# Attention with chunk selection and a gated FFN: key extremes ahead of the transposes, guard and mask as products, and a new order

## The chip, the cores and the metric

One core of a Trainium2 chip runs the whole kernel. The metric is device microseconds (us) of one execution, the lower the better; beside the measured time stands the span that the profiler shows on the core. The engines are PE (TensorE matmul, with its weight load PEld), DVE (VectorE), ACT (ScalarE), POOL (GpSimd) and SP (SyncE, which only issues DMAs here).

## The reference, cut to what matters

For 4 sequences of 768 tokens, 8 heads and 64 channels, each query scores the 24 chunks of 32 keys by an upper bound, keeps the six best, and attends causally to the keys of these chunks. The heads' outputs side by side (512 wide) go through a sigmoid-gated FFN with 1536 hidden units.

```python
k_min = np.min(k_chunks, axis=3)                  # chunks of 32 keys
k_max = np.max(k_chunks, axis=3)
ub = np.sum(np.maximum(q * k_min, q * k_max), axis=-1)      # per query and chunk
ub = np.where(causal, ub, -1000000000.0)          # chunks that begin behind the query
top_chunks = np.argsort(ub, axis=-1)[..., -6:]
scores = scale * np.matmul(q, k.transpose(0, 1, 3, 2))
mask = sel & (pos[:, None] >= pos[None, :])
attn = softmax(np.where(mask, scores, -1000000000.0))
x = (attn @ v).transpose(0, 2, 1, 3).reshape(B * S, H * D)
gate = 1.0 / (1.0 + np.exp(-(x @ w_gate)))
out = (gate * (x @ w_val)) @ w_out
```

## The kernel before, in words

**Stages.** The 3072 tokens go through nine stages. Sequence 0 takes the stages 0 (128 rows), 1 (256) and 2 (384), so that work begins on little data; the sequences 1 to 3 take two stages of 384 rows each (3 to 8). Each stage has a preparation (keys and queries turned so that channels lie on partitions, key extremes, bounds, selection), an attention part (scores, exp, product with v, normalising) and an FFN part.

**Order.** Every operation is a task with a name `kind:stage.number` and one or more engines that may run it. A string `ORDER` lists all tasks by name, with `/1` or `/2` where not the first engine is taken; they are issued in this order, and each engine runs its own instructions in it, as a queue. Buffers are rings of fixed length: `ld` has 6 loads, PSUM has two double banks `big` and four single banks `m`. The numbers in the code behind an engine's name are a planner's costs, which place filler matmuls and nothing else.

**Names.** `kch`, `qch`: loads of 128 keys or queries of sequence 0 (lines 455 and 460, on SP's queue or ACT's). `vn`, `v`: loads and casts of the values. `wst`, `w`: nine loads of the FFN's weights on POOL's queue (507, 509). `ps`: a small DMA that copies 25 pattern rows into the keys, which join the selection to the scores (407). `kTp`, `qT`: four fp32 transposes of 128x128 by PE (561). `kxn`: the minimum or maximum of chunks' keys (571); `kc`: what is left of it, the minimum and the difference to the maximum, into `kcat` (580 to 593). `hk`: keys as f16 into `headK` (604, 611). `Qc`: queries out of PSUM, once raw and once rectified, since the bound is q times minimum plus relu(q) times difference (522 on ACT, 526 on DVE); `hq`: their cast to f16 (537). `ub`: the matmuls of the bounds (733); `ubq`, `mx8`, `Ap`, `apT`, `mq`: causal penalty, the eight largest, the selection as rows of `headQ` (736 to 761). `sc`: scores (810), `at`: exp (815) and POOL's causal select on the diagonal block (821), `pv` (835), `xn` (848), `xtp`, `xT` (861, 866), `gv` gate and value matmuls (891), `gate` (901), `hglu` (903), `o` (917), `osb` (924), `out` (932).

**Stage 0** has only four chunks, so nothing need be selected for its first 128 queries, except where a bound is so large that the check on it, the guard, matters. `first_guard` computes the bounds, the largest bound less a constant (`guard`), transposes it by PE (708) and copies it as eight more rows under the queries (`first`); `firstK` holds the keys with eight constant rows (`less`) under them, so that the score matmul subtracts the guard with its 72 rows.

**Sequences 1 to 3** load keys and queries in 128-byte pieces on SP's queue (`kb`, `qb`, line 422, 192 KB each, four to a transpose). DVE turns them in 32x32 blocks (`kTt` 641, `Qct` 672), reduces (`kn`, `kx`, 646) and writes `kcat` (654, 655); `rl` (681, 683) makes relu of the queries in SBUF.

**Warm-up.** Where PE would wait in the first stages, `fill` (340) puts matmuls on zeros into its queue.

Of the kernel before, what the change touches and what calls it, by code (L numbers as in the profile page):

```python
# [17 lines left out]
LATENCY = {"PE": 0.22, "ACT": 0.08, "DVE": 0.06, "POOL": 0.12, "SP": 3.0, "Q0": 3.0, "Q2": 3.0}  # L18


ORDER = """
    c.0 kch.0 wst0.0 is.0 is.2 qch.0 c.2 w0.0 wst1.0 is.1 vn.0 c.3 vn.1 c.4 c.8/1 v.0 wst2.0 c.5 kTp:0.0 c.6 kch.1
    vn.2 qT:0.0 kxn:0.0 ps.0 kxn:0.1 Qc:0.1 qch.1 kc:0.0 wst3.0 w1.0 Qc:0.3 wst4.0 Qc:0.2 kch.2 hk:0.0 wst5.0 Qc:0.0
    hk:0.1 wst6.0 ubp:0.1 qch.2 hk:0.2/1 ubp:0.0 v.1 kTp:1.0 hk:0.3/1 c.9 qT:1.0 kxn:1.0 Ap:0.1 c.11 c.10 kxn:1.1
    Qc:1.1 wst7.0 w2.0 vn.3 gT:0.1/1 Qc:1.2/1 kTp:1.1 gT:0.0/1 sc:0.1 Qc:1.0/1 sc:0.0 at:0.2 kxn:1.3 Qc:1.3 at:0.3
    kxn:1.2 at:0.0 kc:1.0 qT:1.1 at:0.1 Qc:1.6 pl.0 hk:1.1 wst8.0 pv:0.3 pv:0.2 pv:0.6 pv:0.0 pv:0.1 Qc:1.4 xn:0.0
    w3.0 c.7 Qc:1.7 hk:1.2 xtp:0.0 pv:0.4 pv:0.7 pv:0.5 Qc:1.5 xn:0.1 hk:1.0/1 ub:1.0 Ap:0.0 xtp:0.1 ubq:1.0 hq:1.1
    xT:0.0/1 ubq:1.1 xT:0.1/1 mx8:1.0 hk:1.3/1 gv:0.6 kch.3 v.2 gv:0.0 qch.3 gv:0.7 Ap:1.0 hq:1.0/1 gv:0.1 w4.0 ub:1.1
    gv:0.8 kch.4 apT:1.0 gv:0.3 gv:0.2 gate:0.1 mq:1.3/2 v:0.0 ubq:1.2 sc:1.3 gate:0.0 mq:1.1 qch.4 ubq:1.3 at:1.6
    mx8:1.1 mq:1.0 sc:1.1 mq:1.2 gv:0.4 at:1.2 gv:0.5 Ap:1.1 sc:1.2 kch.5 at:1.4 sc:1.0 at:1.7 apT:1.1 mq:1.7/2 at:1.0  # L30
    mq:1.6/2 sc:1.7 mq:1.4/2 v.3 hglu:0.0 gv:0.9 gv:0.10 qch.5 at:1.14 sc:1.6 w5.0 at:1.3 pv:1.7 gv:0.11 at:1.1
    at:1.12 sc:1.4 at:1.5 pv:1.6 pv:1.1 mq:1.5 at:1.8 pv:1.4 pv:1.3 pv:1.2 pv:1.5 at:1.13 sc:1.5 xn:1.1 pv:1.0 at:1.9
    qT:2.0 at:1.10 at:1.15 hglu:0.1 kTp:2.0 c.13 at:1.11 xn:1.0 pv:1.14 gv:0.12 Qc:2.2 w6.0 gv:0.18 vn.4 gv:0.19
    gv:0.20 kxn:2.1 gv:0.13 c.14 gate:0.3 gv:0.14 vn.5 pv:1.9 pv:1.15 kxn:2.0 pv:1.13 gate:0.2 pv:1.10 pv:1.12 kTp:2.2
    vn.6 xn:1.3 Qc:2.0 kb:3.0 pv:1.8 pv:1.11 qT:2.2 xn:1.2 hk:2.0/1 xtp:1.0 w7.0 Qc:2.8/1 gv:0.15 Qc:2.3 gv:0.21
    xtp:1.1 xT:1.0 hk:2.1/1 gv:0.22 gv:0.23 xT:1.1 gv:0.16 gv:0.17 Qc:2.1 gv:1.0 hglu:0.2 kTp:2.1 gate:1.0 hglu:0.3
    gv:1.2 Qc:2.11 w8.0 kxn:2.2 gv:1.1 Qc:2.9 gv:1.4 hglu:1.0 gate:1.1 qT:2.1 kxn:2.5 gate:1.2 gv:1.12 Qc:2.6 kxn:2.4
    gv:1.3 gv:1.13 gate:1.6 hglu:1.1 Qc:2.5 gv:1.16 hglu:1.6 gv:1.5 kxn:2.3 gate:1.8 gv:1.10 Qc:2.10 gv:1.11 hglu:1.2
    Qc:2.4 gv:1.14 kc:2.0 gv:1.17 gate:1.5 hq:2.0 Qc:2.7 gv:1.18 hglu:1.5 hglu:1.8 gate:1.7 ub:2.0 v.4 gate:1.9 gv:1.6
    ubq:2.0 gv:1.19 kb:3.1 gate:1.3 ubq:2.1 ub:2.1 hk:2.2/1 mx8:2.0 o:0.0 kb:3.2 gv:1.7 hk:2.4/1 v.5 o:0.1 Ap:2.0  # L40
    hk:2.3/1 o:0.2 kb:3.3 o:0.3 apT:2.0 hk:2.5/1 o:0.4 mq:2.0/2 qb:3.0 v.6 o:0.5 hglu:1.9 mq:2.1 ubq:2.2 sc:2.0 mq:2.3
    gv:1.15 qb:3.1 hq:2.1 osb:0.0/1 at:2.0 sc:2.1 hglu:1.3 gv:1.20 at:2.2 qb:3.2 hglu:1.7 sc:2.3 at:2.1 ubq:2.3
    gv:1.21 mx8:2.1 gate:1.10 gv:1.8 qb:3.3 at:2.5 sc:2.2 Ap:2.1 gv:1.9 kb:3.4 gate:1.4 gv:1.22 mq:2.2 hglu:1.10
    at:2.3 sc:2.6 apT:2.1 kb:3.5 gv:1.23 gate:1.11 Qct:3.0 at:2.4 sc:2.4 at:2.9 pv:2.0 mq:2.4 kb:3.6 pv:2.4 pv:2.3
    hglu:1.4 pv:2.2 v:0.1 pv:2.1 at:2.6 sc:2.7 Qct:3.1 mq:2.5 kb:3.7 o:1.6 at:2.10 at:2.11 sc:2.5 kTt:3.0 vn:3.0
    pv:2.5 qb:3.4 o:1.7 at:2.8 xn:2.0 pv:2.11 at:2.7 sc:2.9 qb:3.5 mq:2.6 o:1.8 hglu:1.11 at:2.14 sc:2.8 mq:2.7 o:1.0
    qb:3.6 vn:3.1 at:2.12 pv:2.8 pv:2.9 pv:2.10 kTt:3.1 pv:2.7 sc:2.10 qb:3.7 rl:3.0 at:2.13 o:1.1 kn:3.0 c.12 o:1.9
    hq:3.0 kb:5.0 pv:2.6 pv:2.12 pv:2.13 at:2.15 sc:2.13 pv:2.14 kx:3.0 o:1.10 at:2.20 out:0.0 at:2.16 sc:2.12 kb:5.1
    o:1.11 at:2.18 sc:2.14 xn:2.1 o:1.2 at:2.21 o:1.3 kb:5.2 Qct:3.2 o:1.4 osb:1.1 sc:2.11 kc:3.0 o:1.5 at:2.17 kb:5.3
    sc:2.15 Qct:3.3 at:2.19 ub:3.0 at:2.23 at:2.22 pv:2.19 pv:2.17 qb:5.0 osb:1.0/1 pv:2.16 hk:3.0 pv:2.15 rl:3.1  # L50
    pv:2.20 pv:2.18 ubq:3.0 pv:2.22 pv:2.21 pv:2.23 xtp:2.0 xn:2.2 qb:5.1 hq:3.1 xT:2.0/1 xn:2.3 ubq:3.1 xtp:2.1
# [954 lines left out]
```

## Time and profile before

| | |
|---|---|
| median of three runs | 300.95 us (300.33 to 301.96) |
| the profiled execution | 300.8 us, span 298.8 us |
| granted clock of TensorE | 1.00 |
| busy in the span | PE 284.5, DVE 212.4, ACT 203.9, POOL 107.5 us |

A row of the timeline reads: start, duration (both us), engine, line, operation, output and input by the program's names, and how many instructions it groups; in brackets, the idle time before it and what ended it. Matmuls are pipelined, so that a busy PE isn't always a PE at its peak. A window's row gives start and end, length, then the busy time of each engine with the count of its instructions, the granted clock, the DMA share (the time that packets took on the 16 DMA engines, over the window's; it can pass 1) and GB/s.

### The profile page before, as it was taken

How to read it: one execution, taken by the hardware profiler on the slowest of the kernel's cores; microseconds unless marked ns; L12 is line 12 of the kernel's file. 1: busy time of each engine (PE TensorE's matmuls, PEld its weight loads, DVE VectorE, ACT ScalarE, POOL GpSimd, SP SyncE). 2: the span in 40 equal slices, each digit the busy share in tenths (PEclk: the TensorE clock that was granted, in tenths of full speed). 3: DMA queues.
4: the chain of work that ended last, by engine and by line, in shares of the span. 5: the costliest groups of instructions: out<-in, count | busy, mean ns of one | idle time of the engine just before them, and what ended most of it. 6: DMA issues, size and time to landing. Idle time of an engine off the chain costs nothing.

```text
span 298.8 us, 6823 instructions
## 1 busy us (share of the span) xinstructions
PE 284.5 (95%) x2642; PEld 181.2 (61%) x2642; DVE 212.4 (71%) x581; ACT 203.9 (68%) x299; POOL 107.5 (36%) x175
## 2 busy tenths in 40 slices
PE   6668998999999999999999999999999999999995
...
DMA  7999999999699273575790500006210000021012
GB/s 152 256 218 279 229 171 114 193 149 175 74 215 160 43 141 58 96 63 109 111 85 2 124 0 2 3 3 71 20 70 2 35 2 0 2 103 39 0 70 106
DMA packets 110072, 27.99 MB, mean 94 GB/s; under 512 B 100311, under 2 KB 105525, under 8 KB 110040
## 3 DMA queue, kind: packets, MB, share of 16 engines
q1 hardware_dynamic: 81608, 19.28, 31.5%
...
q10 hardware_dynamic: 1712, 0.66, 1.1%
...
q14 instruction: 12, 0.10, 0.1%
...
## 4 chain that ended last, share of the span: by engine, by line
PE 83%; DVE 8%; DMA 4%; ACT 2%; issue 1%; SPq 1%; DVEq 0%; ACTq 0%
PE m_o L917 21%; PE m_v L891 17%; PE m_g L891 16%; PE big_sc L810 12%; PE m_pv L835 6%; PE big_gv L891 5%; PE m_ub L733 4%; DMA ld_q<-in_q_dram 4%; PE m_xtp L861 2%; ACT Qcat L522 1%; DVE kxn L571 1%; DVE mx L749 1%; PE big_kqT L561 1%; ACT at L815 1%; DVE hglu L903 1%
## 5 line engine op out<-in xcount | busy, mean ns | idle before, releaser
L815 ACT ACTIVATE at<-big_sc 128x1024 f16<-128x1024 f32 (+3 forms) x96 | 84.7, 909 | 17.1 <-PE big_sc L810 11.6
L917 PE MATMUL m_o<-wo,hglu 128*128 128x512 f16 (+1 forms) x300 | 72.0, 370 | 0.0
L821 POOL TENSOR_SCALAR_AFFINE_SELECT at<-at 128x384 f16<-128x384 f16 (+2 forms) x66 | 33.3, 515 | 105.5 <-ACT at L815 101.6
L891 PE MATMUL m_v<-xT,wv 128*128 128x384 f16 (+2 forms) x384 | 71.2, 306 | 0.1
L891 PE MATMUL m_g<-xT,wg 128*128 128x384 f16 (+2 forms) x384 | 70.3, 306 | 0.0
L903 DVE SCALAR_TENSOR_TENSOR hglu<-gate,m_v 128x384 f16<-128x384 f16 (+1 forms) x88 | 44.9, 527 | 19.8 <-PE m_v L891 15.5
L901 ACT ACTIVATE gate<-m_g 128x384 f16<-128x384 f32 (+1 forms) x88 | 40.8, 477 | 24.4 <-PE m_g L891 20.3
L891 PEld LDWEIGHTS <-wg 128*128 128x128 f16 x432 | 38.7, 98 | 23.8 <-issue 4.4
L810 PE MATMUL big_sc<-headQ,headK 89*128 89x128 f16 (+2 forms) x472 | 51.6, 240 | 0.8 <-DVE headQ L761 0.6
L891 PEld LDWEIGHTS <-wv 128*128 128x128 f16 x432 | 38.6, 98 | 20.6 <-issue 0.9
L810 PEld LDWEIGHTS <-headK 89*128 89x128 f16 x472 | 33.4, 97 | 12.7 <-issue 1.1
L917 PEld LDWEIGHTS <-hglu 128*128 128x128 f16 x300 | 27.0, 98 | 22.7 <-issue 1.2
L835 PEld LDWEIGHTS <-at 128*128 128x128 f16 x672 | 30.2, 98 | 12.7 <-issue 1.9
L835 PE MATMUL m_pv<-v,at 128*128 128x65 f16 x672 | 34.0, 194 | 1.1 <-POOL at L821 1.1
L761 POOL COPY headQ<-apT 25x384 f16<-25x384 f16 (+1 forms) x30 | 14.7, 490 | 27.1 <-DVE apT L757 25.6
L672 DVE STREAM_TRANSPOSE Qcat<-ld_qb 64x768 f32<-64x768 f32 x24 | 23.1, 964 | 0.8 <-POOL headQ L537 0.4
L924 ACT ACTIVATE osb<-m_o 128x512 f32<-128x512 f32 (+1 forms) x17 | 9.9, 587 | 18.7 <-PE m_o L917 18.7
L903 DVE SCALAR_TENSOR_TENSOR hglu<-gate,big_gv 128x384 f16<-128x384 f16 x12 | 6.6, 553 | 21.9 <-ACT gate L901 20.7
L848 DVE TENSOR_TENSOR xnat<-m_pv,rz 128x384 f16<-128x384 f32 (+1 forms) x34 | 18.1, 534 | 1.2
L537 POOL CAST headQ<-Qcat 64x1536 f16<-64x1536 f32 (+1 forms) x11 | 15.6, 1419 | 8.8 <-ACT Qcat L522 8.6
L901 ACT ACTIVATE gate<-big_gv 128x384 f16<-128x384 f32 x12 | 5.9, 491 | 17.4 <-PE big_gv L891 17.4
L681 ACT ACTIVATE Qcat<-Qcat 64x1536 f32<-64x1536 f32 x11 | 16.3, 1483 | 0.3
(112 smaller groups left out, 314.4 us busy)
## 6 DMA issues: line engine op xcount, KB each, us to landing
...
```

Source lines behind the costliest of these rows:

```text
L537: copy(tl(("headQ", s), [89, H, st.n], F16)[0:64, h0:h0 + 4, :], tl(("Qcat", s))[0:64, h0:h0 + 4])
L672: nc.vector.transpose(tl(qd, [128, H, HS])[0:64, h:h + 2].rearrange("p a (c t) -> p a c t", t=CH), tl(("ld", "qb", b, u))[64 * e:64 * e + ...
L681: nc.scalar.activation(dst, src, AF.Relu)
L810: nc.tensor.matmul(ps[:, 128 * o:128 * (o + m)], (hk if s else firstK)[0:rows, h, jl:jl + 128], (tl(("headQ", s)) if s else first)[0:rows, ...
L815: add(at(x + 0.03 * t + 0.01), [("ACT", 0.19 + w * 0.815e-3, lambda sc=sc, a=a, w=w: nc.scalar.activation(tl(a, [128, 1024], F16)[:, 0:w], ...
L821: nc.gpsimd.affine_select(out=dg, in_=dg, compare_op=ALU.is_ge, fill=0.0, base=0, pattern=[[0, nd], [1, 128]], channel_multiplier=-1)
L835: nc.tensor.matmul(pvp[:, ib - q0, h % HP, :], tl(a)[:, 128 * o:128 * o + 128], head_v(b, jb // HB)[:, h, jb % HB, :], start=(jb == 0), st ...
L848: nc.vector.tensor_tensor(dst, pvp[:, :, :, 0:64], r.to_broadcast([128, nb, HP, 64]), ALU.mult)
L891: nc.tensor.matmul(ps(i)[:, n * (fb - f0):n * (fb - f0 + 1)], w16[:, c, 128 * fb:128 * fb + 128], tl(("xT", s, c // 2))[:, c % 2, :], star ...
L901: add(at(x) - EV, [("ACT", 0.18 + 0.81 * el, lambda gate=gate, ps=ps: nc.scalar.activation(tl(gate, [128, G * n], F16), ps(0), AF.Tanh, sc ...
L903: add(at(x) - EV, [("DVE", 0.15 + 1.04 * el, lambda gate=gate, hg=hg, ps=ps: nc.vector.scalar_tensor_tensor(tl(hg, [128, G * n], F16), tl( ...
L917: nc.tensor.matmul(tl(o, [128, N]), tl(("hglu", s, fc // G))[:, c0:c0 + 128], wo16[:, fc, cols], start=(fc == 0), stop=(fc == NFB - 1))
```

## The change: what it does

Only sequence 0's stages change in what they compute with, but `ORDER` is new for the whole kernel.

- **Extremes first.** `kxn` is now a reduce over the eight key rows of one partition, from the loaded block in SBUF, ahead of the transposes (two per 128 keys, 12 in all, as before). PE transposes the result (`kxTp`, six fp32 transposes), and `kc` is two reduces from PSUM and a subtraction in place of a copy and three two-input operations.
- **Stage 0's mask and guard** are products summed into the scores in PSUM: one matmul of `ident16` with `later` (the causal penalty) for each half of the heads, and eight of `lessk` with `gT16` (task `sc:0` a second time, `_guarded`). The POOL selects of stage 0, `firstK`, and the copies into it and out of it go; keys are copied straight to `headK`.
- **Stage 0's queries** are cast to f16 and transposed by 16 f16 matmuls into two tiles; one DVE maximum against the column `floor` (a very small number for the raw half, zero for the rectified half) or two ACT operations bring them to `first`.
- **Stages 1 and 2** evict each query tile once (two operations in place of four), and relu is made from SBUF, two operations a stage. Their transposes use the single banks `m` and no `big` bank.
- **Loads.** The first queries move from ACT's queue to SP's, the first values from both queues to ACT's; POOL makes the identity and stage 0's constants ahead of the first weight load and not behind it; value casts are tasks of half a block. `ident16` is copied from `ident32`.
- **Order.** All of `ORDER` is new, with other engines chosen for many tasks: POOL's casts of 64x1536 are 11 for 7, its `mq` copies 33 for 26, DVE's relu operations 4 for 1, `xT` copies on DVE 6 for 3.

```diff
@@ const_tasks @@
-        weight_tasks(0, -97)
-        add(-96, [("POOL", 0.55, lambda: make_identity(nc, ident32))], r=[("wst", 0)], w=["id32"])
-        weight_tasks(1, -92, ["id32"])
...
+        def _later():
+            nc.gpsimd.memset(later, 0.0)
             nc.gpsimd.affine_select(
+                out=later, in_=later, compare_op=ALU.is_ge, fill=NEG,
+                base=0, pattern=[[1, 128]], channel_multiplier=-1)
+        add(-96, [("POOL", 0.55, lambda: make_identity(nc, ident32))], w=["id32"])
+        add(-94, [("POOL", 0.75, _first_stage)], r=["id32"], w=["one"])
...
         def _less(copy):
-            copy(firstK[64:64 + H], less.rearrange("p (h o) -> p h o", o=1).to_broadcast([H, H, 128]))
+            copy(lessk, less.rearrange("p (h o) -> p h o", o=1).to_broadcast([H, H, 128]))
@@ prep_groups @@
-            def _ext(op, i, j=j, kT=kT):
-                nc.vector.tensor_reduce(tl(kxn, [128, 2, nb, 32])[:, i, j].rearrange("p (c h) -> p c h", h=H),
-                                        bank(kT, j, "k").rearrange("p r (c x h) -> p c h r x", h=H, c=4), mybir.AxisListType.XY, op)
+                def _ext(j=j, i=i, op=op):
+                    nc.vector.tensor_reduce(tl(kxn, [128, nb, 128])[:, j, 64 * i:64 * i + 64],
+                                            tl(("ld", "k", s))[:, j].rearrange("p (r d) -> p d r", r=8), mybir.AxisListType.X, op)
...
+            def _kxT(j=j):
+                nc.tensor.transpose(tl(kxT, [128, nb * 128])[:, 128 * j:128 * j + 128], tl(kxn)[:, j], ident32)
...
-            nc.vector.tensor_copy(odd.rearrange("p i (j c) -> p i j c", j=nb), x[64:128])
...
-            nc.vector.tensor_tensor(lo, v4(x[0:64, 1]), v3(odd[:, 1]), ALU.min)
-            nc.vector.tensor_tensor(v3(odd[:, 0]), v4(x[0:64, 0]), v3(odd[:, 0]), ALU.max)
-            nc.vector.tensor_tensor(hi, v3(odd[:, 0]), lo, ALU.subtract)
+            nc.vector.tensor_reduce(lo, x[0:64], mybir.AxisListType.X, ALU.min)
+            nc.vector.tensor_reduce(kx, x[64:128], mybir.AxisListType.X, ALU.max)
+            nc.vector.tensor_tensor(hi, kx, lo, ALU.subtract)
...
+                        for e in range(2):
+                            nc.tensor.matmul(ps[64 * e:64 * e + 64, r], q16[:, c0:c0 + 64], ident16, start=True, stop=True)
...
+                    if eng == "DVE":
+                        nc.vector.tensor_scalar(dst, src, floor, None, ALU.max)
+                    else:
+                        for i, f in enumerate((AF.Copy, AF.Relu)):
+                            nc.scalar.activation(dst[64 * i:64 * i + 64], src[64 * i:64 * i + 64], f)
...
+            def _relu(eng, h0=4 * u):
+                dst, src = tl(("Qcat", s))[64:128, h0:h0 + 4], tl(("Qcat", s))[0:64, h0:h0 + 4]
@@ attn_tasks @@
+                    if s == 0:
+                        nc.tensor.matmul(ps, ident16, later.rearrange("p (o c) -> p o c", o=1).to_broadcast([128, HU, 128]), start=True, stop=False)
...
+                        if s == 0:
+                            nc.tensor.matmul(ps[:, 128 * o:128 * o + 128], hk[0:64, h, 0:128], first[0:64, h, :], start=False, stop=False)
+                            continue
...
+                def _guarded(segs=segs, sc=sc):
+                    for o, h, _, _, _ in segs:
+                        nc.tensor.matmul(tl(sc)[:, 128 * o:128 * o + 128], lessk[:, h, :], gT16, start=False, stop=o == HU - 1)
...
-                if t == 0:
+                if t == 0 and s:
@@ loads @@
-    LOADS = (("SP", "k00", 4.8), ("Q2", "q00", 4.8), ("SP", "v00a", 8.0), ("Q2", "v00b", 8.0), ("SP", "k10", 10.1), ("SP", "q10", 11.7),
-             ("SP", "k11", 13.3), ("SP", "q11", 16.0), ("Q2", "v10", 17.4), ("SP", "v11", 23.8),
...
+    LOADS = (("SP", "k00", 4.9), ("SP", "q00", 6.6), ("SP", "k10", 7.9), ("SP", "q10", 9.4), ("SP", "k11", 10.9), ("SP", "q11",
+             12.3), ("SP", "v11", 20.1), ("Q2", "v00i", 5.6), ("Q2", "v00h", 11.4), ("Q2", "v10", 19.5), ("SP", "k20", 21.8),
...
+    QUEUE = (("w0", 12.5), ("w1", 16.4), ("w2", 20.3), ("p00", 21.0), ("w3", 27.0), ("w4", 31.7), ("w5", 34.8), ("w6", 37.8),
+             ("w7", 40.9), ("w8", 44.0), ("v20", 46.8), ("v21", 48.4), ("v22", 50.2))
```

The numbers behind `LOADS` and `QUEUE` are the planner's landing times. In `ORDER`, around sequence 1's first stage, DVE's transposes stand as `Qct:3.0`, `kTt:3.0`, `Qct:3.1`, `kTt:3.1` (before: `Qct:3.0`, `Qct:3.1`, `kTt:3.0`, `kTt:3.1`), and nine tasks of `o:1` (two matmuls each), 15 matmuls of `pv:2` and two score tasks of stage 2 stand behind `ub:3.0` that stood ahead of it.

532 lines of the change are left out of this document (277 added, 255 removed), and 2 rows, old and new, of the table LOADS.

## The prediction

> **What bounds the kernel now.** I read the page first, then busy time by stretch, then the early chain, the loads and the handover from sequence 0 to sequence 1.
>
> ```profile
> span 298.8 us, 6823 instructions
> PE 284.5 (95%) x2642; PEld 181.2 (61%) x2642; DVE 212.4 (71%) x581; ACT 203.9 (68%) x299; POOL 107.5 (36%) x175
> PE   6668998999999999999999999999999999999995
> DMA  7999999999699273575790500006210000021012
> ```
>
> The tenths show PE at 60 to 80% in the first four slices (7.5 us each), then full until the last. The DMA engines are full for about nine slices. The windows give busy time in each stretch (length; PE, PEld, DVE, ACT, POOL; granted PE clock; DMA share; GB/s):
>
> ```profile
> 0.00:30.00 30.00, 21.30 (x169) 12.71 (x170) 18.79 (x59) 18.56 (x29) 20.06 (x47) 1.00 1.07 227
> 30.00:50.00 20.00, 18.28 (x230) 15.26 (x228) 16.23 (x47) 16.30 (x30) 6.80 (x11) 1.00 1.26 174
> 50.00:80.00 30.00, 29.62 (x331) 19.97 (x329) 27.20 (x88) 25.73 (x34) 17.76 (x27) 1.00 1.06 152
> 80.00:290.00 210.00, 209.93 (x1885) 130.07 (x1884) 148.48 (x386) 141.81 (x205) 62.91 (x92) 1.00 0.38 58
> 290.00:299.00 9.00, 5.38 (x36) 3.22 (x33) 1.67 (x3) 1.47 (x3) 0.00 (x0) 1.00 0.31 112
> ```
>
> And the warm-up matmuls (`fill`, line 340), which compute nothing:
>
> ```profile
> 0.00:10.00 10.00, 5.50 (x13) 1.94 (x14) 1.00 0.89 166
> 10.00:20.00 10.00, 3.17 (x14) 1.08 (x11) 1.00 1.17 252
> 20.00:30.00 10.00, 2.57 (x20) 1.44 (x20) 1.00 1.16 262
> ```
>
> In 0 to 30 us PE is busy 21.30, of which 5.50 + 3.17 + 2.57 = 11.24 is filler: some 10 us of use in 30, so 20 are lost. From 30 to 80 it loses 1.72 + 0.38 = 2.1 us, from 80 to 290 only 0.07. The tail loses 3.6, and the diff leaves its structure (last `o`, `osb`, `out`) alone. So the span is the PE work plus what PE loses before about 70 us. After that PE is a full queue: whatever moves across that border comes back one for one.
>
> **The change part by part.** The border I use is `ub:3.0`, the first matmuls of sequence 1's first stage. In the trace:
>
> ```profile
> 59.06 0.98 DVE L641 STREAM_TRANSPOSE kT_kT<-ld_kb 128x768 f32<-128x768 f32 x1
> 61.69 0.97 DVE L641 STREAM_TRANSPOSE kT_kT<-ld_kb 128x768 f32<-128x768 f32 x1
> 62.70 1.75 DVE L646 TENSOR_REDUCE kn<-kT_kT 128x48 f32<-128x1536 f32 x1
> 64.36 1.74 DVE L646 TENSOR_REDUCE kx<-kT_kT 128x48 f32<-128x1536 f32 x1
> 67.61 0.14 DVE L654 COPY kcat<-kn 64x48 f32<-64x48 f32 x1
> 68.43 0.20 DVE L655 TENSOR_TENSOR kcat<-kx,kn 64x48 f32<-64x48 f32 x1
> 70.11 0.85 PE L733 MATMUL m_ub<-Qcat,kcat 128*32 128x384 f32 x8
> ```
>
> *PE's count.* From the instruction order of both kernels: ahead of `ub:3.0` the new order has 18 matmuls of `o:1`, 15 of `pv:2` and two score tasks fewer. Prices from the chain and the groups:
>
> ```profile
> 50.71 2.16 PE m_o L917 x10
> 52.87 0.39 PE big_sc L810 x6
> 58.37 0.75 PE m_pv L835 x24
> 38.93 0.66 PE big_kqT L561 x4
> ```
>
> 18 x 0.216 = 3.9, 15 x 0.031 = 0.5, two score tasks at 0.39 = 0.8: 5.2 us of real work slide behind the border. New ahead of it are 6 fp32 transposes of extremes (0.66/4 = 0.165 each, 1.0), 16 f16 query transposes and 8 `lessk` products (128 columns or fewer, at about 0.06 = 0.39/6, 1.4) and two mask products of 512 columns (0.216 each, 0.4), less four fp32 transposes of stage 0's queries (0.66): +2.2. The 11 fewer fillers fill idle time only. After the border 298.8 - 70.1 = 228.7 us remain before; so the new span is 228.7 + 5.2 + t = 233.9 + t, with t the start of `ub:3.0`. It breaks even at t = 64.9. The question is whether sequence 1 can be ready 5.2 us sooner.
>
> *The early chain.* What stands behind the 20 lost us:
>
> ```profile
> 3.02 11.39 DMA ld_q<-in_q_dram
> 7.06 1.29 DVE L571 TENSOR_REDUCE kxn<-m_kT 128x32 f32<-128x512 f32 x2 [5.83 <-PE m_kT L561]
> 14.94 0.27 PE L708 MATMUL m_gT<-ident,guard 128*8 128x128 f32 x1
> 19.37 1.25 POOL L821 TENSOR_SCALAR_AFFINE_SELECT at<-at 128x512 f16<-128x512 f16 x2
> 24.56 1.06 PE L891 MATMUL m_g<-xT,wg 128*128 128x128 f16 x16
> 37.22 0.74 DVE L866 COPY xT<-m_xtp 128x512 f16<-128x512 f16 x2
> 0.00:37.96 37.96, 29.16 (x304) 20.36 (x305) 24.98 (x75) 25.21 (x40) 25.40 (x56) 1.00 1.12 227
> 37.96:70.11 32.15, 30.54 (x317) 21.80 (x314) 28.44 (x75) 27.04 (x42) 15.10 (x23) 1.00 1.24 162
> ```
>
> The guard transpose stands at 14.94 because PE's queue is behind the transposes of `q10`, which landed at 3.02 + 11.39 = 14.41. The changed order puts stage 0's chain ahead of those. It also takes the extremes from the key block in SBUF, so that DVE need not wait for the transposes ahead of 7.06 and can start at the landing. No POOL select (2 x 0.63) stands between exp and `pv`; two mask products (0.43 on PE, made ahead of time) and eight guard products (0.5) do instead. Stage 0 saves about 3.5 us: first `gv` near 21 for 24.56. Then DVE rules. It has 24.98 us of work to the end of `xT:1` in before, and idles 13. In after I count 26.6: the same 12 reduces at 0.645, a `lessk` copy, 6 `xn`, 3 key copies, the query maxima (one per tile in place of two ACT evictions) and two chains of bounds. With 2.7 us until its first work and about 3 us of waits (both estimates: 7.06 less transposes and begin, and a quarter of the 13 idle) `xT:1` ends near 32.5 for 37.96: 5.4 us sooner. So its first copy starts near 31.8 for 37.22. From there to `ub:3.0` before takes 70.11 - 37.22 = 32.9 us. Counted as above, PE's work between the transposes of `xT:1` and `ub:3.0` is 31.5 us in before and 29.2 in after: of the 5.2 that left, 2.9 is filled with work that stood ahead of `xT:1` and with the new transposes. So 32.9 - 2.3 = 30.6, plus 1.0 that I allow for new stalls (in the last row above PE lost 32.15 - 30.54 = 1.6): 31.8 + 31.6 = 63.4, span 297.3 (-1.5). Without new stalls it is 62.4, span 296.3 (-2.5).
>
> *The loads of sequence 1.* PE isn't alone. The load tile's rows and the DMA share (last but one column) say:
>
> ```profile
> L422 SPq DMA_DIRECT2D ld_kb<-in_k_dram x4: 900/973/1038, 53.1 to 56.1; - x4
> DMA to landing us min/median/max: 3.4/3.4/5.1
> 20.00:33.00 13.00, 10.75 (x153) 8.24 (x154) 10.83 (x42) 10.76 (x18) 9.67 (x22) 1.00 1.17 256
> 43.00:50.00 7.00, 5.60 (x51) 3.42 (x50) 6.04 (x24) 4.81 (x11) 1.46 (x1) 1.00 0.89 100
> 50.00:60.00 10.00, 10.00 (x108) 7.57 (x106) 9.26 (x30) 7.84 (x13) 5.64 (x10) 1.00 1.13 180
> ```
>
> The second half of the keys is issued from 53.1 to 56.1 and lands 3.4 us (at most 5.1) behind: the last at 59.5 to 61.2. DVE's second transpose starts at 61.69, right after it. The share is at 1.1 to 1.2 nearly throughout, and the bytes are the same in after; changed are only which queue issues the first values and that `w0` comes about 1.2 us later, behind POOL's identity and masks. Same bytes through full engines land at the same time. From landing L the chain on DVE is 0.97 + (1.75 + 1.74, to 3.4 with what overlaps) + 0.96 (67.61 to 68.63) = 5.35 with nothing between. With L = 59.5 to 61.3, `ub:3.0` starts at 64.85 to 66.65. Before, 70.11 - (61.2 + 5.35) = 3.5 us of other DVE work lay between, so this bound was hidden; in after PE arrives at 63.4 and it shows. Span 233.9 + 64.85 to 66.65 = 298.75 to 300.55: -0.05 to +1.75, middle +0.9. I take this bound, the larger of the two.
>
> A rule of the Trainium skill bears on the load reorder: DMA: Bandwidth & Descriptors, section on arbitration, says that each engine takes turns between its queues packet by packet, and that spreading transfers over more issuing engines adds no bandwidth. By it, moving the first values to ACT's queue gains the later loads nothing, and the sum stands at 300 rather than 297.3. The share of 1.17 with 256 GB/s while three queues are active agrees.
>
> *POOL and DVE.* The new order gives POOL more of the casts and copies (casts of 64x1536 go from 7 to 11, `mq` from 26 to 33) and takes them from ACT.
>
> ```profile
> 44.89 1.46 POOL L537 CAST headQ<-Qcat 64x1536 f16<-64x1536 f32 x1 [8.60 <-ACT Qcat L522]
> 44.89 1.63 DVE L591 TENSOR_TENSOR kcat<-kmx,kcat 64x96 f32<-64x96 f32 x1
> 9.04 0.21 DVE L591 TENSOR_TENSOR kcat<-kmx,kcat 64x32 f32<-64x32 f32 x1
> ```
>
> The first two start together and end together within 0.2 us; the operation that took 0.21 on a third of the columns took 1.63. So a cast costs a DVE operation that meets it up to about 1.3 us. In 80 to 290 DVE is busy 148 of 210, so I cost these at nothing there: DVE's slack is the cover. Where it is gone, in 50 to 80 (27.20 of 30), two casts cost 2.6 us. They could gain there too, since ACT, at 25.73 of 30, is relieved.
>
> The Trainium skill, SBUF — State Buffer, section on its two sides, says that VectorE and GpSimd share a port pair under a lock held for the whole instruction. The trace agrees, with 1.63 beside 1.46; by this rule alone the added casts would cost, not save.
>
> *At nothing:* half as many query evictions in stages 1 and 2, with the relu made in SBUF (0.6 to 0.7 each saved, four of 1536 columns added): ACT and DVE, under PE from 38 us on. `m` tiles in place of `big` for the transposes: hidden, unless four `m` buffers run out ahead of the gate matmuls.
>
> **Forecast and rivals.** The sum is for the profiled execution: span 298.8, its time 300.8 (2.0 around it), against a median of 300.95. My forecast, span 298.8 + 0.9 = 299.7, is 301.7. A difference within 0.5% (1.5 us) is about what a measurement of this kernel can't tell from no change.
>
> *Rival 1, faster.* The loads aren't the bound: they land earlier, since DMA has gaps (0.89 in 43 to 50), which a stream that starts without the first values would use. Then PE's own sum holds: -1.5 to -2.5, 298.3 to 299.3. For it: the gap of some 0.8 us, and lost PE time of 20 us that this change aims at. Against: the share of 1.1 to 1.2 on either side.
>
> *Rival 2, slower.* DVE's queue is blocked at the handover. A query transpose of sequence 1 (`Qct:3.0`, line 672) stands ahead of the key transposes, as before, but DVE reaches it sooner and waits for the sixth load; behind it are `hglu` operations that PE needs, and ACT's relu with the exps of stage 2 behind that. A load that lands 3 us late (L = 63, by `w0`'s delay and packets of the pattern rows) holds all of it: t = 63 + 5.35 = 68.35, span 302.3, 304.3. It decides from L = 61.3 on, where each us is one of span. POOL's casts in that stretch have the same price (2.6) and the same place. For it: DVE at 27.20 of 30 and the lock; against: the DMA share of 1.13 in 50 to 60 leaves these loads back to back, with nothing else to delay them.
>
> *Rival 3, it doesn't do what it says.* Stage 0's chain ends no sooner, because its key block or first values land later in the new load order: `xT:1` stays at 37.22, and 37.22 + 31.6 = 68.8 gives a span of 302.7, a time of 304.7. Each us of the 5.4 that fails to come is one from 63.4 up, hidden until 65.8 by the loads' bound; so it shows when less than 3 come. Against: `q10` at 14.41 no longer stands ahead of the guard.
>
> **Chances.** Forecast 0.43, of which a little lies above +1.5; rival 1 0.25, of which a little lies inside 0.5%; rival 2 0.25; rival 3 0.07. Faster 0.23, within 0.5% 0.42, slower 0.35. The forecast's own range is 300.7 to 302.5. For 8 in 10 it goes down to 298.2, just under rival 1, and up to 304.5, by the price of rivals 2 and 3.
>
> **What would show it.** Right: `xT:1` ends at 31 to 34; first `gv` near 21; `ub:3.0` starts 0.1 to 0.3 us behind `kcat`, and that 5.3 to 6 us behind the last `ld_kb`, with PE idle ahead of it by 1 to 3 us; 80 to 290 still full. Wrong: `ub:3.0` at 63.5 or sooner without PE idle (rival 1), or key blocks that land after 62, with DVE waits over 1 us at line 672's transpose (rival 2), `xT:1` at 35 or later (rival 3), or new PE idle after 80 us.

## The result and the profile after

The changed kernel takes 308.66 us (median of four runs, 308.58 to 309.17) against 300.64 for the kernel before: a ratio of 1.0264, with a 95% interval of 1.0227 to 1.0301. It is slower by 8.0 us. Ratios here leave disturbed runs out, so one can differ from the quotient of the medians beside it; the profile of experiment 6 is of such a run. The forecast was 301.7 and the range ended at 304.5.

The page of the changed kernel first: the span, the busy times, and PE, the granted clock and DMA in tenths.

```profile
span 306.9 us, 6851 instructions
...
PE 287.4 (94%) x2659; PEld 182.9 (60%) x2659; DVE 217.8 (71%) x583; ACT 188.0 (61%) x277; POOL 115.9 (38%) x185
...
PE   5774889999999999999999999998999999999995
...
PEclk9799599999999999999999999999999999999999
DMA  8999999998999285051920080023050010010032
```

The loss is again in the first slices, and the line of the granted clock (PEclk) has changed: 7 and 5 where the kernel before had 9 throughout. The windows of the changed kernel:

```profile
25.00:30.00 5.00, 1.49 (x22) 1.30 (x20) 4.94 (x9) 1.78 (x3) 0.00 (x0) 1.00 1.19 256
30.00:35.00 5.00, 2.92 (x28) 2.60 (x28) 0.94 (x2) 1.41 (x2) 3.12 (x7) 0.63 1.34 215
35.00:40.00 5.00, 4.95 (x65) 4.60 (x63) 2.60 (x9) 3.19 (x6) 3.94 (x10) 0.69 1.09 181
...
80.00:290.00 210.00, 208.08 (x1872) 128.47 (x1870) 150.37 (x400) 132.49 (x196) 73.35 (x106) 1.00 0.37 53
```

From 25 to 35 us PE, ACT and POOL stand still for more than half the time (4.41, 3.19 and 3.12 busy of 10), and the clock is at 0.63 behind it. From 80 to 290 PE now loses 1.92 us, where it lost 0.07. The chain of waits in the first 45 us of the changed kernel says what they stood for:

```profile
4.11 8.76 DMA ld_q<-in_q_dram
...
12.88 17.94 DMA ld_v<-in_v_dram
...
30.95 0.02 POOL v L496
...
31.62 0.41 POOL headQ L794
...
32.08 0.69 PE big_sc L848 x4
```

and its waits up to 80 us (waiter, releaser, us in total, times, longest):

```profile
POOL v L496 <- DMA ld_v<-in_v_dram: 7.9, 1, 7.9
PE big_sc L848 <- POOL headQ L794: 5.6, 1, 5.6
```

The second block of values (`v10`, 256 KB) is issued at 12.88, behind the landing of `q11`, and lands at 12.88 + 17.94 = 30.82. Before, it was the first of ACT's two value loads, issued at 1.51 and landed 10.1 us later, at 11.6; the rows of the kernel before (the second gives engine, count, size and time to landing):

```profile
1.51 1.23 ACTq L460 DMA_DIRECT2D ld_v<-in_v_dram  x2
```

```profile
ld_v<-in_v_dram ACTq DMA_DIRECT2D x1, 256.0 KB, 10.1
```

In the changed kernel its cast stands in POOL's queue ahead of the copies of the selection (`mq`), so POOL waits 7.9 us, stage 1's scores wait for the copies, and PE waits 5.6. The wait at 12.88 is of the program, not of ACT: the loads that SP and ACT issue use eight completion semaphores (the counters that say a load has landed) in turn, in program order, and `v10` now stands as the sixteenth, eight behind `q11`, so that its issue waits until `q11` has landed, at 4.11 + 8.76 = 12.87. Before, it stood among the first eight and waited for nothing.

The two marks of the prediction, in the changed kernel's timeline:

```profile
41.01 0.40 DVE L910 COPY xT<-m_xtp 128x512 f16<-128x512 f16 x1
...
71.21 0.85 PE L766 MATMUL m_ub<-Qcat,kcat 128*32 128x384 f32 x8
```

`xT:1` starts at 41.0 (before 37.2, forecast 31.8) and `ub:3.0` at 71.2 (before 70.1, forecast 65.8). By the prediction's sum the span is 233.9 + 71.2 = 305.1; with the 1.85 us that PE newly loses behind 80 us it is 306.95, and 306.9 was measured. The sum holds, and two of its terms were wrong: of the 7.2 us above the forecast span of 299.7, the start of `ub:3.0` makes 5.4 (71.2 for 65.8) and the loss behind 80 us 1.85.

### The profile page after: what moved, and what is told of

The parts are those of the page before. It is cut to its first block, busy times and chain, and to the rows that moved or that the text cites. A ratio compares the mean times of both kernels' runs of the same rounds, so it can differ in the third digit from the quotient of the medians.

```text
span 306.9 us, 6851 instructions
## 1 busy us (share of the span) xinstructions
PE 287.4 (94%) x2659; PEld 182.9 (60%) x2659; DVE 217.8 (71%) x583; ACT 188.0 (61%) x277; POOL 115.9 (38%) x185
## 3 DMA queue, kind: packets, MB, share of 16 engines
q1 hardware_dynamic: 81224, 19.41, 31.6%
## 4 chain that ended last, share of the span: by engine, by line
PE 82%; DMA 9%; DVE 4%; ACT 1%; SPq 1%; issue 1%; POOL 0%; DVEq 0%; POOLq 0%
PE m_o L961 20%; PE m_v L935 17%; PE m_g L935 16%; PE big_sc L848 12%; PE m_pv L879 7%; DMA ld_v<-in_v_dram 6%; PE big_gv L935 5%; PE m_ub L766 4%; DMA ld_q<-in_q_dram 3%; PE m_xtp L905 1%; SPq L472 1%; DVE kxn L570 1%; DVE hglu L947 1%; DVE kcat L690 1%; ACT gate L945 0%
## 5 line engine op out<-in xcount | busy, mean ns | idle before, releaser
L961 PE MATMUL m_o<-wo,hglu 128*128 128x512 f16 (+1 forms) x300 | 73.4, 370 | 1.0 <-DVE hglu L947 1.0
L935 PE MATMUL m_g<-xT,wg 128*128 128x384 f16 (+2 forms) x384 | 71.3, 307 | 0.9 <-ACT headK L603 0.7
L947 DVE SCALAR_TENSOR_TENSOR hglu<-gate,m_v 128x384 f16<-128x384 f16 (+1 forms) x88 | 45.6, 531 | 32.2 <-PE m_v L935 28.4
L865 POOL TENSOR_SCALAR_AFFINE_SELECT at<-at 128x384 f16<-128x384 f16 (+1 forms) x64 | 32.0, 510 | 95.2 <-ACT at L859 82.6
L848 PEld LDWEIGHTS <-headK 89*128 89x128 f16 x472 | 34.7, 99 | 19.0 <-issue 7.8
L879 PEld LDWEIGHTS <-at 128*128 128x128 f16 x672 | 30.6, 99 | 11.7 <-issue 2.1
L794 POOL COPY headQ<-apT 25x384 f16<-25x384 f16 (+1 forms) x38 | 18.5, 487 | 34.2 <-DVE apT L790 28.5
L696 POOL CAST headK<-kT_kT 64x1536 f16<-64x1536 f32 x11 | 16.0, 1458 | 2.7 <-DVE kT_kT L676 2.2
L455 POOL DMA_DIRECT2D v<-in_v_dram x18 | 16.6, 928 | 0.3 <-PE m_v L935 0.3
```

The lines of the kernel that those rows point to most:

```text
L455: nc.gpsimd.dma_start(dst[:, :, i, :], v[b, :, r0 + 128 * i:r0 + 128 * i + 128].rearrange("h p d -> p h d"))
L794: copy(tl(("headQ", s), [89, H, st.n], F16)[64:89, h, :], tl(apT)[32 * i:32 * i + 25, :])
L848: nc.tensor.matmul(ps[:, 128 * o:128 * (o + m)], hk[0:89, h, jl:jl + 128], tl(("headQ", s))[0:89, h, 128 * (ib - q0):128 * (ib - q0 + m)], ...
L865: nc.gpsimd.affine_select(out=dg, in_=dg, compare_op=ALU.is_ge, fill=0.0, base=0, pattern=[[0, nd], [1, 128]], channel_multiplier=-1)
L879: nc.tensor.matmul(pvp[:, ib - q0, h % HP, :], tl(a)[:, 128 * o:128 * o + 128], head_v(b, jb // HB)[:, h, jb % HB, :], start=(jb == 0), st ...
L935: nc.tensor.matmul(ps(i)[:, n * (fb - f0):n * (fb - f0 + 1)], w16[:, c, 128 * fb:128 * fb + 128], tl(("xT", s, c // 2))[:, c % 2, :], star ...
```

## The experiments

Each is the changed kernel with edits, unless it says otherwise. Times are medians of four runs (12 is a single one); ratios are to the kernel before on the same chip. Rows and times inside a run are of its one profiled execution, and four executions of one kernel differ by up to 4.7 us here, so its time is given where it lies far from the median.

**1. The values early.** In `ORDER`, the issue of `v10` (`is.2`):

```diff
-    kch.0 is.1 c.0 c.2 is.0 c.3 qch.0
+    kch.0 is.1 c.0 c.2 is.0 is.2 c.3 qch.0
...
-    Qc:0.0 qT:1.0 is.2 wst3.0
+    Qc:0.0 qT:1.0 wst3.0
```

> The changed kernel with the issue of the second block of values (v10) moved in the order to stand right behind the two issues of the first values on ACT's queue. In the changed kernel it stood behind a wait for an older load and was issued at 12.88 us, landing at 30.82; POOL's cast of it held POOL's queue, PE waited 5.59 us and its granted clock fell to 0.63 to 0.69. Theory A (the late values are the loss): it is issued near 2 us and lands before 17, the 5.59 us gap and the low clock between 30 and 40 us go, ub:3.0 starts at 65.5 to 67 instead of 71.2, and the time is 302 to 304 us. Theory B (the new order with its other engines loses by itself, the gap only moves the loss to another place): 306 us or more. Theory C (stage 0's products and early extremes do gain and only the load hid it): below 300 us.

Measured: 308.05 us, ratio 1.0261 (1.0213 to 1.0309). `v10` landed at 13.95 and the 5.6 us wait was gone, but of the 8 us hardly anything came back. `xT:1` started at 37.6, `ub:3.0` at 68.5; the profiled execution, 306.43 us, was the best of the four. Taken alone, theory A failed by its number, and theory B's number came true: other losses stood close behind this one. The nearest to `ub:3.0` is the second half of sequence 1's keys. DVE waited 1.74 us for them, and `ub:3.0` came 5.2 us behind:

```profile
63.26 0.98 DVE L676 STREAM_TRANSPOSE kT_kT<-ld_kb 128x768 f32<-128x768 f32 x1 [1.74 <-DMA ld_kb<-in_k_dram]
```

In the changed kernel these keys had landed by 60.6. POOL, no longer held, now issued the two value loads of sequence 1 at 56.2, before the keys had landed, and not at 59.7; experiments 8 and 9 take this up. Close behind stand a subtraction that took 1.73 us beside a cast of POOL, and a low clock behind PE's wait for it:

```profile
17.20 1.73 DVE L585 TENSOR_TENSOR kcat<-kmx,kcat 64x64 f32<-64x64 f32 x1
```

```profile
20.00:25.00 5.00, 4.38 (x37) 2.44 (x37) 3.75 (x19) 4.05 (x6) 2.36 (x5) 0.61 1.14 249
25.00:30.00 5.00, 4.79 (x52) 4.39 (x52) 4.27 (x18) 3.26 (x7) 1.30 (x4) 0.71 1.18 254
```

**2. The cast later, the load as late as it is.**

```diff
-    kch.5 vs.6 kxn:2.0
+    kch.5 kxn:2.0
...
-    at:1.14 pv:1.1 sc:1.3 Qc:2.0 w4.0 at:1.5 at:1.6 mq:1.5 Qc:2.1 pv:1.5
+    at:1.14 sc:1.3 Qc:2.0 w4.0 at:1.5 at:1.6 mq:1.5 Qc:2.1 vs.6 pv:1.1 pv:1.5
```

> The changed kernel with POOL's cast of v10 moved behind the selection copies and selects that it held up, right ahead of the first product with these values, which moves behind the score task next to it; the load is as late as before. Theory A1 (the landing at 30.8 is the bound, since the products with the values wait for it in PE's queue): PE gets 1 to 2 us more of scores done in the gap, 306.5 to 308 us. Theory A2 (POOL's blocked queue is the loss, not the landing): PE goes on without the values and the time falls to 304 or below.

Measured: 307.28 us, ratio 1.0230 (1.0196 to 1.0264), as theory A1 said; A2 failed. The interval meets that of the changed kernel (1.0227 to 1.0301), so a gain in time is not shown. In the profiled execution (306.18, the best) the values landed at 30.7 as before; PE's wait fell to 3.5 us, now at the products, and `xT:1` came at 38.0. So both parts show in the trace: the landing holds the products, and the cast in POOL's queue held the scores besides.

**3. The kernel before, with late values.** `is.2` moved from second place on ACT to behind stage 1's second query eviction, where it too waits for an older load.

```diff
-    c.0 kch.0 wst0.0 is.0 is.2 qch.0
+    c.0 kch.0 wst0.0 is.0 qch.0
...
-    Qc:1.2/1 kTp:1.1
+    Qc:1.2/1 is.2 vn.2 kTp:1.1
```

> The kernel before with its issue of v10 moved on ACT's queue from second place to behind the queries of stage 1 and the first guard copy (issued near 15 us for 1.51). Theory A: the values land at 27 to 32 us for 11.6, PE waits some us at stage 1's scores or products, and the time is 304 to 308 us. Theory B (before's order isn't sensitive to that load): within 1.5 us of 300.6.

Measured: 309.34 us, ratio 1.0286 (1.0237 to 1.0336). Issued at 15.86, `v10` landed at 32.98; `xT:1` moved from 37.2 to 46.3 and `ub:3.0` from 70.1 to 79.2 (in the slowest execution of the four, 310.47). Theory A held, with a loss larger than its 304 to 308: a late `v10` alone makes the kernel before as slow as the changed one.

**4. Fillers in the gap.** The planner is told that `v10` lands at 31.0:

```diff
-    ("Q2", "v10", 19.5)
+    ("Q2", "v10", 31.0)
```

> The changed kernel with the planner told that v10 lands at 31.0 us and not at 19.5, which changes only its filler matmuls: more of them where PE would wait. The load stays late. Theory A with a clock part: the granted clock stays at 1.00 in 25 to 40 us, where it was 0.63 to 0.69 over some 7.9 us of PE work, and the time falls by 2 to 3 us to about 306. Rival: PE is held by DVE and ACT in these stretches anyway, and the clock costs under 1 us: 308 to 309.

Measured: 309.77 us, ratio 1.0316 (1.0263 to 1.0368). The clock was 1.00 from 25 to 40 us, yet `xT:1` came at 40.5 and `ub:3.0` at 71.4. While the values are what all wait for, the clock behind the gap costs nothing that shows at `ub:3.0` (71.2 in the changed kernel). The rival held, 0.8 us above its 308 to 309.

**5 to 8. On top of the early values.** Half reduces, more fillers, one cast of POOL moved, and the three together. The kernels with half reduces (5, 8 and 9) leave half the keys out of the extremes:

```diff
# 5
-    tl(("ld", "k", s))[:, j].rearrange("p (r d) -> p d r", r=8), mybir
+    tl(("ld", "k", s))[:, j].rearrange("p (r d) -> p d r", r=8)[:, :, 0:4], mybir
# 6
-    ... t - since > 0.5:   (t - since - 0.05, ...)   fill(int(0.7 * o[0] ...
+    ... t - since > 0.2:   (t - since + 0.3, ...)   fill(int(1.0 * o[0] ...
# 7
-    apT:1.0 hq:1.1 pl.0 ... wst6.0 ubq:1.2
+    apT:1.0 pl.0 ... wst6.0 hq:1.1 ubq:1.2
# 8: all three
```

> The kernel with the early issue of v10, and each of the 12 key extremes reduced over four of the eight key rows of a partition (it leaves half the keys out of the extremes, so the selection is another). From SBUF the reduce took 1.04 us for 0.69 from PSUM before; on half the data it should take 0.55 to 0.65. Theory D (DVE's queue sets xT:1): the 11 reduces ahead of it save 4 to 5 us of DVE work, xT:1 starts at 33 to 35 for 37.6, ub:3.0 at 64.5 to 66 for 68.5, and the time falls by 2.5 to 4 us against the kernel with early values. Theory P (PE with its low clock, or ACT, sets it): under 1 us.

> The kernel with the early issue of v10 and more filler matmuls in stages 0 and 1: the planner puts them in waits over 0.2 us (for 0.5) and makes them 0.3 us longer. Its granted clock was 0.75 in 5 to 10, 0.61 in 20 to 25 and 0.71 in 25 to 30 us; it should be near 1.00. Theory P (the low clock is on the chain): xT:1 starts 1.5 to 2.5 us sooner and the time falls by as much. Theory D (DVE's queue sets xT:1 and hides a slow PE): under 1 us either way.

> The kernel with the early issue of v10, and POOL's second cast of stage 1's queries moved behind its next copy and weight issue, so that it doesn't run beside kc:1.0, whose subtraction took 1.73 us beside it at 17.20 (0.27 in the changed kernel, where it ran alone). Theory L (the shared port costs this chain): the subtraction takes 0.3 us, ub:1.0 starts 1.3 to 1.5 us sooner, the clock doesn't fall at 20 us, and xT:1 and the time gain 1 to 3 us. Rival: the cast meets another DVE operation or delays a copy by as much, and the time changes by less than 0.7 us.

> The last three edits together on the kernel with the early issue of v10 (it too leaves half the keys out of the extremes). Theory D, P and L together: xT:1 at 31 to 33 us as forecast, and then the loads of sequence 1 are the bound, ub:3.0 at 65 to 66 us, the span 301 to 302, of which 1.9 are waits after 80 us that the new order has and the old had not. Rival (the forecast's bound by the loads doesn't exist): ub:3.0 at 63 or sooner, span 297 to 299.

Measured:

| kernel | time, us | ratio (95% interval) | profiled run, us | `xT:1` | DVE turns the keys (its wait) | `ub:3.0` |
|---|---|---|---|---|---|---|
| 1, early values | 308.05 | 1.0261 (1.0213 to 1.0309) | 306.43 | 37.6 | 63.3 (1.7) | 68.5 |
| 5, half reduces | 307.91 | 1.0230 (1.0170 to 1.0291) | 309.48 | 33.5 | 64.2 (2.9) | 70.4 |
| 6, fillers | 309.03 | 1.0233 (1.0156 to 1.0309) | 310.48 | 35.4 | 64.7 (4.7) | 70.0 |
| 7, cast moved | 308.13 | 1.0236 (1.0171 to 1.0301) | 309.09 | 38.3 | 65.4 (3.2) | 70.7 |
| 8, all three | 306.95 | 1.0217 (1.0162 to 1.0273) | 309.22 | 32.8 | 64.3 (4.6) | 69.5 |

Theory D was right on `xT:1`: half the reduce brings it 4.1 us sooner. Theory P said the same of the fillers: with a clock of 1.00 from 5 to 40 us, 6 has it 2.2 us sooner, but in its slowest execution. Better evidence is kernel 10 below, which has the fillers and the moved cast and starts it at 35.8 for 37.6 in 1: 1.8 us for the two. In 7 the subtraction took 0.26, but the clock was 0.50 from 15 to 25 us, for a reason that was not looked into, so that this run tells nothing of the lock's price. And all were wrong on the time: with `xT:1` at 32.8, one us from the forecast, `ub:3.0` was still at 69.5. In all five kernels DVE waited for the keys, and `ub:3.0` came 5.2 us behind their transpose (6.2 in 5). In kernel 8 the loads of sequence 1's second half of keys (issues and landing; then DVE, PE and POOL in the timeline) were late:

```profile
L436 SPq DMA_DIRECT2D ld_kb<-in_k_dram x4: 838/1493/2468, 53.6 to 59.2; - x4
DMA to landing us min/median/max: 4.7/5.5/6.3
```

```profile
52.59 1.77 POOL L455 DMA_DIRECT2D v<-in_v_dram  x2
64.25 0.98 DVE L676 STREAM_TRANSPOSE kT_kT<-ld_kb 128x768 f32<-128x768 f32 x1 [4.61 <-DMA ld_kb<-in_k_dram]
69.49 1.19 PE L766 MATMUL m_ub<-Qcat,kcat 128*32 128x384 f32 x4 [3.56 <-DVE kcat L690]
```

DVE waited 4.61 us for the keys, which landed at 64.1, and 5.2 us later PE began: the bound that the forecast rested on, but with the keys 4 us later than it took them. POOL, now earlier, had issued two value loads of sequence 1 at 52.6, which before went out at 60 and 62.5, and they share the DMA engines with the keys. (The profiled execution of 8 is 2.3 us above its median; how late the keys were in the others isn't on record.)

**9 to 11. The value loads behind the keys.** 9 is 8 with these two loads moved; 10 is the same with full reduces, so the changed kernel with four repairs; 11 also moves the last weight load (and, for the planner, its landing time).

```diff
# 9, 10, 11
-    sc:2.3 vn:3.0 kTt:3.0 ... gv:1.18 vn:3.1 hglu:1.2 ... kx:3.0 hk:3.1
+    sc:2.3 kTt:3.0 ... gv:1.18 hglu:1.2 ... kx:3.0 vn:3.0 vn:3.1 hk:3.1
# 11
-    pv:1.11 wst8.0 w5.0 ... mq:2.5 hglu:1.10
+    pv:1.11 w5.0 ... mq:2.5 wst8.0 w8.0 hglu:1.10
```

> The kernel with the last three edits (early v10, half reduces, fillers, moved cast), and POOL's two value loads of sequence 1 (vn:3.0, vn:3.1) moved from 52.6 us to behind its next select near 60 us. With the three edits xT:1 starts at 32.8 us, as forecast, but the second half of sequence 1's keys lands at 64.12 instead of 60.3, and ub:3.0 starts at 69.5 = 64.1 + 5.4. Theory V (these value loads, issued ahead of the keys because POOL is now earlier, take the DMA engines from them): the keys land at 59.5 to 60.5, ub:3.0 starts at 65 to 66, and the time is 3.5 to 4.5 us less, a profiled span near 303 and a time of 303 to 304.5 us. Rival (the keys are late by the engines' total bytes): they land at 63 or later, and the time changes by under 1 us.

> As the run with the values later, but with the extremes over all eight rows, so the whole computation of the changed kernel with four repairs. Theory D with V: xT:1 starts 2.5 to 3 us later (35 to 36), PE reaches ub:3.0 at 66 to 67, near the loads' bound, and the time is within 1.5 us of the run with half reduces, 303.5 to 306 us. Rival (the reduces are the main loss): 4 us slower than that run.

> As that, and the last weight load (w8, 512 KB, first used near 59 us) moved on POOL's queue from 31 us to behind a copy near 55 us, so that sequence 1's keys need not share the DMA engines with it. Theory of the loads' bound: the keys land 2 to 3 us sooner (57 to 58), and if PE is ready, ub:3.0 starts up to 2 us sooner and the time is 302 to 304 us. Rival 1 (PE's own queue behind xT:1 is the bound by now): under 0.7 us of gain. Rival 2: the first output products wait for w8, 1 to 3 us slower.

Measured: 9 takes 304.70 us, ratio 1.0141 (1.0114 to 1.0167); 10 takes 304.40, ratio 1.0134 (1.0104 to 1.0164); 11 takes 306.37, ratio 1.0187 (1.0166 to 1.0208). The rows are of kernel 10: loads, then the timeline.

```profile
L436 SPq DMA_DIRECT2D ld_kb<-in_k_dram x4: 879/972/1024, 53.6 to 56.7; - x4
DMA to landing us min/median/max: 3.3/3.4/3.5
```

```profile
60.58 1.78 POOL L455 DMA_DIRECT2D v<-in_v_dram  x2
60.19 0.98 DVE L676 STREAM_TRANSPOSE kT_kT<-ld_kb 128x768 f32<-128x768 f32 x1 [0.43 <-DMA ld_kb<-in_k_dram]
64.65 1.34 DVE L689 COPY kcat<-kn 64x48 f32<-64x48 f32 x1
64.49 1.46 POOL L696 CAST headK<-kT_kT 64x1536 f16<-64x1536 f32 x1
66.54 1.27 PE L766 MATMUL m_ub<-Qcat,kcat 128*32 128x384 f32 x8 [0.48 <-DVE kcat L690]
```

Theory V held on the keys: they land at 60.1 and DVE starts on them at once. 9 gains 2.25 us on the median of 8, where 3.5 to 4.5 were expected; the profiled spans, 307.4 and 302.6, differ by more, since 8's is of its slowest execution. From the landing to `ub:3.0` it takes 6.4 us and not 5.35, because a copy that took 0.14 in the kernel before takes 1.34 beside a cast of POOL. 9 and 10 have the same `ub:3.0`, 66.5: the dear reduces delay `xT:1` by 2.8 us (33.0 to 35.8) and nothing behind it, since the loads end later. In 11 the keys landed at 57.9, but DVE came to them at 59.7 and `ub:3.0` at 66.0, and the kernel was 2 us slower. The load that came late was the next one, the second half of sequence 1's queries:

```profile
70.83 0.97 DVE L707 STREAM_TRANSPOSE Qcat<-ld_qb 64x768 f32<-64x768 f32 x1 [2.60 <-DMA ld_qb<-in_q_dram]
```

They were issued from 55.5 to 63.3, beside the 512 KB of weights issued at 55.5, and landed 9.3 to 9.9 us behind their issue, where it was at most 5.6 in kernel 10. Behind DVE's 2.6 us PE waited 1.1 and 0.7. So rival 2 had the size and not the cause: the weights had landed at 63.4, and no product waited for them. The contention moved from the keys to the queries.

**12. The reduce by itself.** The kernel before with 16 reduces of 128x512 f32 behind its end, where POOL has no work: eight forms, each twice, of which six are shown:

```diff
+    pr: 128x512 f32 in SBUF;  probe: the same in PSUM;  each line twice
+    nc.vector.tensor_reduce(pq, pr.rearrange("p (r d) -> p d r", r=8), X, max)         # L983
+    nc.vector.tensor_reduce(pq, pr.rearrange("p (d r) -> p d r", r=8), X, max)         # L984
+    nc.vector.tensor_reduce(pq[:, 0:32], pr.rearrange("p (r d) -> p d r", r=16), X, max)  # L985
+    nc.vector.tensor_reduce(pq[:, 0:32], pr.rearrange("p (d r) -> p d r", r=16), X, max)  # L986
+    nc.vector.tensor_reduce(pq, probe.rearrange("p (r d) -> p d r", r=8), X, max)      # L987
+    nc.vector.tensor_reduce(pq[:, 0:32], probe.rearrange("p (r d) -> p d r", r=16), X, max)  # L988
```

> The kernel before with 16 more reduces of 128x512 f32 on DVE behind its last output, which measure the disputed reduce by itself with POOL idle: source in SBUF or PSUM, 64 outputs of 8 or 32 outputs of 16, the reduced elements side by side or 256 bytes apart. Theory S (the source or its stride makes the 1.04 us): the strided SBUF forms take 1.0 and the PSUM forms 0.69 with the same outputs. Rival O (the number of outputs makes it): 64 outputs take 1.0 us from both, 32 outputs 0.65 to 0.7 from both. Rival P (the port shared with POOL makes it): all take 0.7 with POOL idle.

The timeline of DVE behind the end:

```profile
295.72 1.01 DVE L983 TENSOR_REDUCE pq<-pr 128x64 f32<-128x512 f32 x1
296.76 0.69 DVE L984 TENSOR_REDUCE pq<-pr 128x64 f32<-128x512 f32 x1
297.49 1.01 DVE L985 TENSOR_REDUCE pq<-pr 128x32 f32<-128x512 f32 x1
298.53 0.69 DVE L986 TENSOR_REDUCE pq<-pr 128x32 f32<-128x512 f32 x1
299.32 0.69 DVE L987 TENSOR_REDUCE pq<-probe 128x64 f32<-128x512 f32 x1
300.04 0.69 DVE L988 TENSOR_REDUCE pq<-probe 128x32 f32<-128x512 f32 x1
```

Theory S held. The count of outputs doesn't matter, and POOL, which is idle here, isn't needed: from SBUF with the reduced elements 256 or 128 bytes apart it takes 1.01, side by side 0.69, and from PSUM 0.69 even far apart. The two forms not shown have the access of the kernel before (over two axes) and say the same: 0.69 from PSUM (L989) and 1.01 from SBUF (L990).

**13. A late cast moved.** Kernel 10 with one more of POOL's casts moved:

```diff
-    o:5.2 hglu:5.9 hq:8.0 o:5.3 ... gv:6.12 hk:8.0
+    o:5.2 hglu:5.9 o:5.3 ... gv:6.12 hq:8.0 hk:8.0
```

> The kernel with four repairs and full reduces (early v10, fillers, two casts and value loads of POOL moved), and one more of POOL's casts, hq:8.0, moved behind the selects of stage 7, away from kc:8.0 near 204.6 us, whose subtraction took 1.37 us beside it for 0.20 alone; behind it an hglu was late and PE waited 1.00 us at 207.3. Theory L (the port's lock makes this stall): the subtraction takes 0.2 to 0.5 us, the 1.00 us wait goes, PE's loss from 80 to 290 us falls from 1.93 to about 0.9, and the span is 0.8 to 1.0 us shorter than 302.7. Rival (the cast meets the next operation, or hglu is late by DVE's length anyway): the loss stays above 1.6 us.

The place in the changed kernel, and the same subtraction and the loss of PE in 13:

```profile
208.71 1.46 POOL L551 CAST headQ<-Qcat 64x1536 f16<-64x1536 f32 x1 [0.74 <-DVE Qcat L707]
208.87 1.37 DVE L690 TENSOR_TENSOR kcat<-kx,kn 64x48 f32<-64x48 f32 x1
211.55 0.82 PE L961 MATMUL m_o<-wo,hglu 128*128 128x512 f16 x3 [0.99 <-DVE hglu L947]
```

```profile
205.10 0.20 DVE L690 TENSOR_TENSOR kcat<-kx,kn 64x48 f32<-64x48 f32 x1
```

```profile
80.00:290.00 210.00, 209.00 (x1872) 128.85 (x1871) 148.02 (x384) 129.88 (x192) 72.69 (x105) 1.00 0.36 54
```

Measured: 304.11 us, ratio 1.0113 (1.0090 to 1.0136), span 302.2 for 302.7. The subtraction takes 0.20, PE's wait of 1.0 us is gone, and its loss from 80 to 290 us falls from 1.93 to 1.00. Theory L held on the stall and gave half of the 0.8 to 1.0 us that it expected of the span; the 0.3 us between the medians of 13 and 10 is inside their spread.

**14. The values late again.** Kernel 10 without the edit of experiment 1.

> The kernel with four repairs, but with the issue of v10 back where the changed kernel has it, so that it lands near 30 us: this prices the late values by themselves, when nothing else hides them. Theory A: PE's wait of 5 us or more at stage 1's scores comes back, xT:1 starts at 39 to 41 us for 35.8, ub:3.0 at 69.5 to 71 for 66.5, and the time is 3 to 5 us more than 304.4. Rival (the loads' bound behind it hides them): less than 1 us more.

Measured: 309.67 us, ratio 1.0300 (1.0260 to 1.0341). The waits of PE in this kernel:

```profile
PE big_sc L848 <- POOL headQ L794: 4.5, 1, 4.5
```

`xT:1` came at 41.4 for 35.8, `ub:3.0` at 72.1 for 66.5, and the time is 309.67 - 304.40 = 5.3 us more, a little above the 3 to 5 expected. Theory A held, by the size that experiment 1 alone couldn't show. The issue that waits (at 13.81) also holds ACT's queue, but this is not the price: ACT's first `gate` comes at 25.52 for 25.29. No version beat the kernel before; 13 is the best of the new order, 3.4 us behind it.

## Why the prediction was wrong, point by point

**The step that failed first: the early chain.** The prediction had `xT:1` start at 31.8, and it came at 41.0. It asked what the load reorder does to `w0` and to the queue of the first values, and said that nothing else changed. It had not asked when `v10` is issued: every DMA of ACT's queue, with the older load that its issue waits for, belonged in the count. In the repaired kernel this is worth 5.3 us (experiment 14); taken out alone it gave back only 0.6 (experiment 1), so the 8.0 us do not split into prices that add up. On `xT:1` they do: kernels 14, 10 and 9 start it at 41.4, 35.8 and 33.0, so that of the 9.6 us above the forecast 5.6 are the late values, 2.8 the reduces, and 1.2 stay open. Rival 3 had the outcome in kind, `xT:1` not sooner, but gave it a chance of 0.07, a time of 304.7 and different loads as the reason.

**The reduces.** "The same 12 reduces at 0.645" took the price of a PSUM source for a source in SBUF with 256 bytes between the elements. They cost 1.00 to 1.05 us:

```profile
25.37 1.05 DVE L570 TENSOR_REDUCE kxn<-ld_k 128x64 f32<-128x512 f32 x1
```

Eleven before `xT:1` make about 11 x (1.03 - 0.69) = 3.7 us of DVE work (an estimate). With half reduces, fillers and early values `xT:1` came at 32.8, so the rest of the count was right within 1 us. On the end of the kernel the reduces cost nothing (9 against 10), as the loads hid them. The Trainium skill, SBUF — State Buffer, in a note in the section Door 1: The DMA port swizzle, says that SBUF is read in lines of 16 bytes, and that each access which crosses to a new line pays a penalty. The probe's 1.01 against 0.69 agrees with it for DVE; the prediction did not weigh it.

**The fillers.** "The 11 fewer fillers fill idle time only" was wrong on the clock, which fell to 0.63 and 0.69 behind the gap; but that cost nothing while the values were late (experiment 4). With early values, the fillers and the moved cast brought `xT:1` 1.8 us (kernel 10 against 1).

**From `xT:1` to `ub:3.0`.** The forecast was 31.6 us; the changed kernel took 71.2 - 41.0 = 30.2. This term was near (the forecast had 30.6 without the 1.0 allowed for stalls). The border holds too: with the 5.2 us of work behind it the sum above comes within 0.1 us of the measured span.

**The bound by the loads.** In the changed kernel it wasn't the bound: its keys were issued by 57.0 and landed in at most 3.6 us, and DVE, held by the late chain, turned them at 64.9. In kernel 10 it was: 60.1 + 6.4 = 66.5, for 65.8 in the forecast. "Same bytes through full engines land at the same time" failed once POOL was early, from experiment 1 on: in kernel 8 the keys landed at 64.1, the price of rival 2 (L = 63), but by value loads of sequence 1, which the prediction hadn't priced.

**POOL's casts.** They were costed at nothing behind 80 us. One of them made 0.99 us of the 1.9 (experiment 13), and another 1.1 us of the handover in kernel 10. The price of a meeting, "up to 1.3 us", was near (1.2 us at both places, 1.5 in experiment 1), and the cover was not: DVE's idle time over 210 us says nothing of the place where the meeting falls. The rule of the Trainium skill quoted with the prediction (SBUF — State Buffer, on the two sides) agrees with both places: 1.37 and 1.34 us beside casts of 1.46. That the cast makes the second one was not tested. The rest of the 1.9, a wait of 0.6 and one of 0.2 for ACT's gate at 115 and 120 us in kernel 10, was not tested.

**What stays open.** Kernel 13 is still 3.4 us behind. About 0.9 of it is the loss after 80 us, and 66.8 - 64.9 = 1.9 is `ub:3.0` behind the prediction's break-even. What the mask and guard products are worth alone was not isolated: first `gv` came at 23.15 for 24.56, 1.4 sooner where 3.5 were forecast.
